# Buffers taken when free, filled waits, and a mask factor on VectorE in place of mask matmuls, in a sparse attention and expert kernel

## The chip, the cores and the metric

The kernel runs on one core of one Trainium2 chip. The metric is the device time of one execution in microseconds (us). Runs that are 1.5 to 3.5% longer than the fastest of the kernel, mostly with a lower granted TensorE clock, are classed as slow and left out of every ratio below.

## The reference, cut to what matters

There are 4 batches, 8 heads, 768 positions, head size 64. Attention is local (a window of 15 positions to either side) plus one entry for each block of 32 keys, whose key is the maximum of the block and whose value is its mean. Its output, 768 x 512 for each batch, goes through a layer of 8 experts; one expert is chosen for a whole batch.

```python
mask_l = np.abs(pos[:, None] - pos[None, :]) < window          # window = 16
scores_l_m = np.where(mask_l, scores_l, -1000000000.0)
scores_all = np.concatenate([scores_l_m, scores_s], axis=-1)    # scores_s: 24 block entries
a = np.exp(scores_all - np.max(scores_all, axis=-1, keepdims=True))
a = a / (np.sum(a, axis=-1, keepdims=True) + 1e-09)
attn = np.matmul(a, np.concatenate([v, v_sum], axis=2))
...
logits = x.mean(axis=1) @ w_gate          # one row for a batch
e_idx = np.argmax(logits, axis=1)         # one expert for a batch
...
h = np.maximum(x[mask] @ w1[e], 0.0)
out[mask] = gate_w[mask, None, None] * (h @ w2[e])
```

Two things follow for the schedule. A batch's expert is known only when its whole attention is done, because the router takes the mean over all positions; only then can that expert's weights (2 MB as they land) be fetched. And a masked score may be made zero after exp as well as very negative before it.

## The kernel before

The program does not issue its work in the order in which it is written. It registers operations with an assumed duration, a priority, the operations they depend on and the buffers they take. A small scheduler, `solve`, plays them through and fixes one order for each engine. That order is what is compiled. A buffer is the oldest in a ring:

```python
for s in op.takes:
    h = hist[s.pool]
    if len(h) >= self.bufs[s.pool]:
        old = h[-self.bufs[s.pool]]            # the one taken longest ago
        if any(u.end is None for u in old.users):
            ok = False
            break
        r = max(r, max(u.end + self.LAT[u.eng] for u in old.users))
```

A score group is one pair of heads and one half of the positions. Four mask matmuls write the bias (0 or -30000) into PSUM, and twelve score matmuls add to it. There are 8 groups for each batch, and one score buffer of two PSUM banks for all:

```python
sc = sc_pool.tile([128, 2, 512], FP32, name="sc", tag="sc")
...
for i, (bias, cs) in enumerate(parts):           # 2 parts x 2 heads = 4 matmuls
    for hh in range(2):
        nc.tensor.matmul(sc[:, hh, cs], lhsT=bias[rs, :], rhs=ident6[rs]...[:, cs],
                         start=i == 0, stop=False, tile_position=(hh * D, 0))
for w in range(NW):                              # 6 windows x 2 heads = 12 matmuls
    for hh in range(2):
        nc.tensor.matmul(sc[:, hh, w * QB : (w + 1) * QB], lhsT=ka[rs, pr, j, :],
                         rhs=qT[rs, j * QB : (j + 1) * QB],
                         start=False, stop=w == NW - 1, tile_position=(hh * D, 0))
```

ScalarE takes the exp (`S_exp`), TensorE multiplies by the values (`O_mm`, tile `ops`), VectorE normalises (`O_norm`), TensorE transposes (`X_mm`, tile `xps`) and ScalarE copies out and sums each row (`X_out`). When all eight groups of a batch are through, the router (`G_mm`, tile `lgps`) multiplies these sums by the gate weights in sixteen matmuls. The expert is `H_mm` (tile `hps`) and `Y_mm` (tile `o_ps`). `V_sum` (tile `vsps`) makes the block means of V; no value product of a batch can run before it.

Before everything else come nine matmuls of zeros (`first_warm`), which are meant to warm the clock. Sixteen transposes took 0.85 us right behind them, at 5.28 us, and 0.53 us at 6.86.

The softmax here doesn't subtract the row's maximum and nothing guards it: scores larger than these inputs give would overflow.

## Time and profile before

| | |
|---|---|
| median of 3 runs (range) | 176.25 us (173.95 to 177.74) |
| profiled run, its span | 175.92 us, 174.2 us |
| granted clock, whole span | 0.901 |
| state of the profiled run | slow |
| fast runs of this kernel in the later calls | 171.4 to 174 us |

TensorE is the engine to look at: it is 87% busy, and the stages in which it is not are the place where something other than its own work decides. The lines of this profile are shown in the prediction.

### The profile page before, as it was taken

What the parts mean: (1) busy time and instruction counts of PE and PEld (TensorE: products, weight loads), DVE (VectorE), ACT (ScalarE), POOL (GpSimd) and SP (SyncE); (2) the same over time, 40 slices, a digit from 0 to 9 for tenths busy, and PEclk for the clock granted to TensorE, in tenths of its full rate; (3) what the DMA queues carried; (4) which work ended last, traced back from release to release, by engine and by line L of the source; (5) the groups of instructions that cost most, each with busy time, mean ns of one, the idle gap of its engine ahead of it and who ended that gap; (6) DMA issues with size and microseconds to landing.
All of it is one profiled execution on the core that took longest, in us unless ns stands there. A gap on an engine that the chain in (4) does not pass through costs nothing.

```text
span 174.2 us, 5138 instructions
## 1 busy us (share of the span) xinstructions
PE 151.6 (87%) x2214; PEld 93.2 (53%) x2225; DVE 83.1 (48%) x224; ACT 100.9 (58%) x204; POOL 45.9 (26%) x62
## 2 busy tenths in 40 slices
PE   6627887495857999989999999999999999999990
PEld 2316766374644555735665657456666544565440
DVE  5991997593396235750885258508644300100000
ACT  2134687677438366866495668563977533485341
POOL 6998300002990009164000090000000370000000
PEclk9965589855597599999999999999999999999999
DMA  3999999990999999999999999981300099990333
GB/s 48 139 138 196 167 206 183 150 56 4 123 161 202 207 194 148 143 198 221 255 245 220 185 147 196 207 234 64 124 0 6 0 122 196 281 243 4 120 121 120
DMA packets 60038, 26.03 MB, mean 149 GB/s; under 512 B 42608, under 2 KB 56944, under 8 KB 60016
## 3 DMA queue, kind: packets, MB, share of 16 engines
q0 software_dynamic: 56032, 19.40, 114.8%
q1 hardware_dynamic: 3984, 6.31, 10.5%
q8 instruction: 17, 0.28, 0.7%
q14 instruction: 5, 0.04, 0.1%
HBM read 38.81 MB, written 6.29 MB: 259 GB/s over the span
## 4 chain that ended last, share of the span: by engine, by line
PE 77%; DVE 12%; ACT 4%; issue 4%; POOL 1%; DVEq 0%; POOLq 0%; ACTq 0%
PE hps L589 25%; PE o_ps L617 24%; PE tps L300 7%; PE sc L411 5%; PE ops L452 4%; PE xps L482 4%; DVE vblk L390 4%; PE sc L423 4%; PE vsps L369 3%; ACT aT L438 3%; DVE xs L469 2%; DVE kmx L328 1%; DVE bind L286 1%; DVE kaug L341 1%; PE lgps L505 1%
## 5 line engine op out<-in xcount | busy, mean ns | idle before, releaser
L589 PE MATMUL hps<-xT,w_sb 128*128 128x384 bf16 x256 | 47.5, 337 | 0.0
L617 PE MATMUL o_ps<-w_sb,hT 128*128 128x512 bf16 x181 | 42.9, 380 | 1.0 <-issue 0.6
L438 ACT ACTIVATE aT<-sc 128x768 bf16<-128x768 f32 x32 | 25.9, 810 | 23.8 <-PE sc L423 23.8
L552 POOL DMA_DIRECT2D w_sb<-in_moe_w_dram x16 | 12.0, 762 | 89.6 <-PE hps L589 53.0
L589 PEld LDWEIGHTS <-w_sb 128*128 128x128 bf16 x256 | 24.4, 101 | 15.9 <-issue 1.5
L608 ACT ACTIVATE hT<-hps 128x384 bf16<-128x384 f32 x53 | 25.2, 492 | 12.7 <-PE hps L589 12.6
L617 PEld LDWEIGHTS <-hT 128*128 128x128 bf16 x192 | 17.4, 98 | 19.4
L636 ACT ACTIVATE o_sb<-o_ps,gcol 128x512 f32<-128x512 f32 x21 | 14.4, 687 | 17.4 <-PE o_ps L617 12.7
L469 DVE TENSOR_TENSOR xs<-ops,rv 128x384 bf16<-128x384 f32 x32 | 17.8, 558 | 1.3
L491 ACT ACTIVATE xT<-xps 128x384 bf16<-128x384 bf16 x32 | 15.5, 493 | 4.9 <-PE xps L482 4.5
L423 PE MATMUL sc<-qT,kaug 64*128 64x64 bf16 x384 | 12.8, 205 | 3.5 <-DVE kaug L347 2.9
L188 POOL DMA_DIRECT2D vblk<-in_v_dram x10 | 15.7, 1576 | 0.5 <-DMA vblk<-in_v_dram 0.5
L606 DVE TENSOR_SCALAR hT<-hps 128x384 bf16<-128x384 f32 x11 | 6.1, 558 | 19.7 <-PE hps L589 19.5
L328 DVE TENSOR_REDUCE kmx<-kaug 128x24 bf16<-128x768 bf16 x16 | 15.0, 947 | 0.9 <-ACT kaug L310 0.9
L411 PE MATMUL sc<-ident,mbias 64*128 64x320 bf16 x64 | 11.2, 346 | 3.3 <-ACT aT L438 3.2
L390 DVE COPY vblk<-vs_sb 24x1536 bf16<-24x1536 bf16 x16 | 11.8, 735 | 4.2 <-ACT vs_sb L310 3.7
L482 PE MATMUL xps<-identb,xs 128*128 128x128 bf16 x96 | 11.1, 245 | 2.9 <-DVE xs L469 2.9
L423 PEld LDWEIGHTS <-kaug 64*128 64x128 bf16 x384 | 9.6, 106 | 5.7 <-issue 3.9
L310 ACT COPY kaug<-tps 128x768 bf16<-128x768 bf16 x11 | 8.8, 799 | 6.3 <-PE tps L300 6.3
L452 PE MATMUL ops<-vblk,aT 120*64 120x65 bf16 x384 | 10.6, 208 | 2.0 <-ACT aT L438 1.4
L300 PE MATMUL tps<-identb,q_nat 96*64 96x96 bf16 x256 | 8.9, 230 | 3.4 <-issue 2.2
L452 PEld LDWEIGHTS <-aT 120*64 120x64 bf16 x384 | 8.6, 121 | 5.3 <-issue 2.3
(74 smaller groups left out, 146.6 us busy)
## 6 DMA issues: line engine op xcount, KB each, us to landing
w_sb<-in_moe_w_dram POOLq DMA_DIRECT2D x12, 512.0 KB, 12.1
out_dram<-o_sb SPq DMA_DIRECT2D x24, 256.0 KB, 5.4
vblk<-in_v_dram POOLq DMA_DIRECT2D x6, 576.0 KB, 21.7
k_nat<-in_k_dram POOLq DMA_DIRECT2D x3, 768.0 KB, 15.3
q_nat<-in_q_dram POOLq DMA_DIRECT2D x3, 768.0 KB, 18.2
vblk<-in_v_dram POOLq DMA_DIRECT2D x2, 564.0 KB, 18.0
w_sb<-in_moe_w_dram POOLq DMA_DIRECT2D x8, 128.0 KB, 5.0
w_sb<-in_moe_w_dram POOLq DMA_DIRECT2D x4, 256.0 KB, 5.9
```

Of the source, the lines that this page charges most:

```text
L300: nc.tensor.transpose(ps[hh * D : (hh + 1) * D, r, :], src[:, 2 * pr + hh, r * D : (r + 1) * D], identb[0:PR, 0:PR],)
L328: nc.vector.tensor_reduce(out=kmxs[b, pr].rearrange("q (j c) -> q j c", c=QB // BLK), in_=kaugs[b % 2][:, pr, :, R_OWN:R_POST].rearrange(" ...
L390: nc.vector.tensor_copy(vblks[b % NV][R_SUM:NR, 2 * pr : 2 * pr + 2, :, 0:D], vss[b, pr][BLK * pr : BLK * pr + NB] .unsqueeze(2) .to_broad ...
L411: nc.tensor.matmul(sc[:, hh, cs], lhsT=bias[rs, :], rhs=ident6[rs].rearrange("p w c -> p (w c)")[:, cs], start=i == 0, stop=False, tile_po ...
L423: nc.tensor.matmul(sc[:, hh, w * QB : (w + 1) * QB], lhsT=ka[rs, pr, j, :], rhs=qT[rs, j * QB : (j + 1) * QB], start=False, stop=w == NW - ...
L438: nc.scalar.activation(aT, scs.pop((b, pr, u))[:, :, 0:HB], ACT.Exp, scale=SCALE)
L452: nc.tensor.matmul(ops[w * QB : (w + 1) * QB, t, hh, :], lhsT=aT[0:NR, hh, c0 : c0 + QB], rhs=vb[0:NR, 2 * pr + hh, u * NW + 2 * t + w, 0 ...
L469: nc.vector.tensor_tensor(out=xs, in0=ops[:, :, :, 0:D], in1=rv.unsqueeze(3).to_broadcast([128, NW // 2, 2, D]), op=ALU.mult,)
L482: nc.tensor.transpose(xps[:, t * 128 : (t + 1) * 128], xs[:, t], identb)
L589: nc.tensor.matmul(hps[:, 0:HB], lhsT=w1_sb[:, dt, ft * 128 : (ft + 1) * 128], rhs=xT[b][:, dt, u * HB : (u + 1) * HB], start=(dt == 0), s ...
L608: nc.scalar.activation(dst, hps[:, 0:HB], ACT.Relu)
L617: nc.tensor.matmul(o_ps, lhsT=hTs[b][:, ft, st * 128 : (st + 1) * 128], rhs=wts[b][1][:, ft, :], start=(ft == 0), stop=(ft == NFT - 1),)
```

## The change

The intent is to take work off TensorE where it is full and to keep its clock up where it is not.

1. In batches 1 to 3 the four mask matmuls of a group go. VectorE multiplies the result of exp by a 0/1 factor instead; two such factors are built once.
2. A buffer is the one that comes free first, and each has its own name.
3. Where the schedule expects TensorE to wait within the first 60 us, matmuls of zeros fill the wait.
4. The router adds its half sums on VectorE first and needs 8 matmuls in place of 16. Batch 1's transposes are held until batch 0's last scores, and some of the assumed durations are new.

```diff
     def solve(self):
-                    h = hist[s.pool]
-                    if len(h) >= self.bufs[s.pool]:
-                        old = h[-self.bufs[s.pool]]
+                    best = None
+                    for i, old in enumerate(held[s.pool]):
+                        if old is None:
+                            t = 0.0
+                        elif any(u.end is None for u in old.users):
+                            continue
+                        else:
+                            t = max(u.end + self.LAT[u.eng] for u in old.users)
+                        if best is None or t < best[0]:
+                            best = (t, i)
 ...
+            op.spare = st - max(room, free.get(eng, 0.0))
 ...
+    def factors(op):                       # seven instructions on VectorE
+        nc.vector.tensor_copy(d_k, it_k)
+        nc.vector.tensor_tensor(out=d_k, in0=d_k, in1=d_k, op=ALU.mult)
+        for i in range(2):
+            nc.vector.tensor_scalar(out=seen[i], in0=d_k, scalar1=float(HALO * HALO),
+                scalar2=None, op0=ALU.is_lt)
 ...
+    def S_mask(b, pr, u):
+        def f(op):
+            rows = aTs[b, pr, u][0:R_SUM]
+            nc.vector.tensor_tensor(out=rows, in0=rows,
+                in1=seen[u].rearrange("p w c -> p (w c)").unsqueeze(1).to_broadcast(
+                    [R_SUM, 2, HB]), op=ALU.mult)
 ...
-            for i, (bias, cs) in enumerate(parts):
+            for i, (bias, cs) in enumerate(parts if b == 0 else []):
 ...
-                        start=False,
+                        start=b > 0 and w == 0,
 ...
+    def G_add(b):                          # reds = the two halves of red, added
 ...
-            for i in range(2 * NP):
+            for i in range(NP):
 ...
+    def warm(op, tile_):
+        if op.start < WARM_UNTIL:          # 60.0
+            for _ in range(int((op.spare - 0.1) / 0.17)):
+                nc.tensor.matmul(tile_, lhsT=zb[:, 0:128], rhs=zb[:, 0:HB],
+                                 start=True, stop=True)
 ...
-        slow_until=24.0, slow=1.8,
+        slow_until=24.0, slow=1.2,
 ...
-    KQ, VV = 1.2, 2.4
+    KQ, VV = 1.1, 2.15
 ...
+        later = [R["S", 0, NP - 1, 1]] if b == 1 else []
 ...
+                if b:
+                    R["e", b, pr, u] = add(
+                        ("dve", 0.5), S_mask(b, pr, u), w - 10, [e, R["fact"]])
```

(The diff is cut to its core. `warm` is called at the head of six of the TensorE operations.)

## The prediction

> **What bounds the kernel now.** I read the busy shares and the 40 slices first, then the chain of work that ended last, then a table of stretches, then the timeline and the DMA issues of the first 62 us. The slices (4.36 us each) show two different kernels:
>
> ```profile
> PE 151.6 (87%) x2214; PEld 93.2 (53%) x2225; DVE 83.1 (48%) x224; ACT 100.9 (58%) x204; POOL 45.9 (26%) x62
> ...
> PE   6627887495857999989999999999999999999990
> ...
> PEclk9965589855597599999999999999999999999999
> DMA  3999999990999999999999999981300099990333
> ```
>
> From about 56 us on TensorE (PE) is at 9 in nearly every slice and its granted clock is full: this part is a sum of PE work. Before that, PE is neither full nor at full clock. The table of stretches (columns: busy us of PE, weight loads, VectorE, ScalarE and GpSimd, each with its count, then granted clock, DMA busy share times length, GB/s) says the same:
>
> ```profile
> 0.00:40.00 40.00, 28.59 (x609) 20.88 (x609) 29.90 (x79) 21.73 (x40) 17.12 (x29) 0.75 1.66 140
> 40.00:62.00 22.00, 16.71 (x291) 11.06 (x288) 11.56 (x32) 12.02 (x29) 9.60 (x10) 0.68 1.00 147
> 62.00:174.20 112.20, 106.35 (x1320) 61.27 (x1329) 41.66 (x114) 67.17 (x136) 19.13 (x23) 1.00 1.17 153
> ```
>
> In the chain (start, us, what) three places matter. One is the serial loop score matmuls, exp, next scores; "L411" are the mask matmuls, "L423" the scores, "L438" the exp. The other two are the same group at full clock, and the router (L505), with which a batch's expert is chosen and its weights may be fetched:
>
> ```profile
> 41.47 0.77 ACT aT L438
> 42.28 0.50 PE sc L411 x4
> 42.78 0.34 PE sc L423 x12
> 43.14 0.82 ACT aT L438
> ...
> 44.82 1.43 PE vsps L369 x36
> 46.28 0.30 DVE vs_sb L312
> ...
> 86.40 0.27 PE sc L411 x4
> 86.67 0.18 PE sc L423 x12
> ...
> 97.74 0.48 PE lgps L505 x16
> ```
>
> There is one score buffer (two PSUM banks), so masks and scores cannot start before the exp has read it. Cold, a turn takes 43.14 - 41.42 = 1.72 us: masks 0.50, scores 0.34, exp 0.81 and hand-overs. Warm, the masks cost 0.27 and the scores 0.18.
>
> The router of batch 0 runs at 39.5 to 40.1 us in the timeline. The expert's first weights are issued at 42.4, its first matmul runs at 46.9, and PE is full from 56. So I split the span as 40.1 us up to the first router and 134.1 us after it. Of the latter, the 40 to 62 stretch has 22.0 - 16.7 = 5.3 us of idle PE, and some 11 us of its busy time ran at half clock, which loses another 5.5 us: about 10.8 us that is not needed work.
>
> [...] the twelve score matmuls take 0.32 to 0.34 us where the granted clock is 0.50 (40 to 46 us) and 0.17 to 0.18 us where it is 1.00. [...] from 36 to 40 us, mostly transposes, PE was busy 4.00 of 4.00 us with a clock of 0.50. [...]
>
> [...]
>
> [...] the 128x176 copies that take 0.20 us later took 1.47 us between 10.6 and 12.1 us, while GpSimd was issuing the V load.
>
> **The change part by part.**
>
> *Mask matmuls.* Four per group, 32 groups before; after, only batch 0's eight groups keep them (the instruction order has 16 + 16 left of 64 + 64). Batches 2 and 3 (16 groups) lie in the saturated part: 16 x 0.27 = 4.3 us. I count 0.20 a group instead, as the mask streams covered some of the twelve weight loads of the scores (0.24 us a group): 16 x 0.20 = 3.2 us.
>
> *Router.* The two half sums are added on VectorE first (about 0.15 us), so 16 matmul passes become 8: 0.24 us off each of the three routers in the saturated part, 0.7 us.
>
> *Batch 1's scores.* These sit in the serial loop. A turn loses its masks: 1.72 becomes about 1.25 us cold, less if warm. In the new order three groups stand ahead of V's sums, all behind the router; in the old one five do, two before the router and three behind it. So V's sums (44.8 us) move earlier with the router and by about another microsecond, and with them the V copies and normalisations that kept PE waiting at 50 to 55 us.
>
> *Fills.* 39 zero matmuls of 128x384, counted in the order: 33 before the first router, six between the third score group of batch 1 and V's sums. At 0.17 us each warm (0.32 cold) they are 6.6 us of PE time (up to 12.5), but each stands where PE is expected to wait anyway. If the waits are as long as planned they cost nothing, and keep the clock up.
>
> *Buffers taken when free, and the order.* Each buffer has its own name now, chosen when it comes free, so a short-lived tile no longer waits for the oldest in the ring. In the profile PE hardly waits for a PSUM buffer by itself; the gain is in the order that this permits. Batch 1's transposes stand after batch 0's last scores. In the old order a q transpose of batch 1 stood before batch 0's last O group and its last two transposes, and PE stood still for 2.2 us before it (31.6 to 33.8), with nothing named that it waited for. The load of q had landed at about 30.2 (13.9 + 16.3), so I suspect the instruction supply behind a full DMA queue, and it may come again.
>
> *VectorE's extra work.* 24 mask products, 24 x 0.47 = 11.3 us; seven instructions that build the factors, about 2 us[...]. They stand ahead of the first copies of K's edges, on the path to the first scores (13.1 us). One more index pattern on GpSimd (the like one took 0.48 us) delays every later load by 0.5. Against it, VectorE loses the first q copy (0.86). I expect the first scores at 13 to 14.5 us: nothing gained, up to 1.4 lost.
>
> *The first router.* V's second half landed at 23.2 us (10.3 + 12.9), q of batch 1 at 30.2; with 0.5 added, 23.7 and 30.7. After V: sums 0.8, copy to SBUF and spread 1.8, then four normalisations of 0.75, a transpose and a copy out, which gives 31. The new order puts all four q transposes of batch 1 (0.46 us each warm, 0.85 cold) before the router: 30.7 + 1.9 to 3.4 + about 1 for what follows, so 33.5 to 36. I take 35.0 in place of 39.5: 4.5 us.
>
> *After it.* Weights landed 3.7 us after issue, issue 2.4 after the router: expert work can start at about 42 rather than 46.9. Its loads take some 11 us more, in which PE has sixteen expert groups and batch 1's rest. Of the 10.8 us lost I expect 7 to remain (about 4 idle, 3 cold): 3.8 us.
>
> *Given back.* In the saturated part O now waits for exp and then VectorE, and VectorE goes from 0.37 busy (41.66 of 112.2) to about 0.45. That is slack enough; I allow 1 us of new idle PE.
>
> Sum: 3.2 + 0.7 + 4.5 + 3.8 - 1.0 = 11.2 us. Span 174.2 - 11.2 = 163.0; the run of that profile took 175.92, so 1.7 is added: 164.7, say 164.5 us.
>
> **The rivals.** (a) *Only PE work counts*: the start stays as it is, because the loads (DMA at 9 in the slices up to 37 us) set the first router, and the gain is 3.2 + 0.7 plus a little: 171. For it: the q load lands at 30 whatever is done. Against: nine microseconds lie between that landing and the router. (b) *VectorE becomes the bound of batch 1*: eight products, the V copies (4.0 us in a row at 46.6), eight normalisations and K's maxima come to some 17 us between 36 and 53; each product also lengthens exp to O. PE would wait about as it does at 50 to 55 now, and the gain shrinks to 7: 168. (c) *The fills are misplaced*: waits are shorter than planned or the clock is cold, and they push real work by up to 6 us, half of it on the path: 168. (d) *The clock stays full from 13 us on*, all slack but 4 us goes: 159.5.
>
> **Range and chances.** 164.5 us, 159 to 170. The saturated part's gain is nearly sure and alone makes over 2% (below 172.7) almost; the start adds to it in all but (a). Faster by over 2%: 0.92; within: 0.07; slower: 0.01.
>
> **What would show it.** Right: the router of batch 0 before 37 us, score groups of twelve matmuls and no masks from batch 1 on, turns of 1.25 us or less, clock above 0.75 in the first 40 us, expert matmuls from 42, PE full from about 50, the product near 0.47 us, router matmuls 0.24. Wrong: a router at 39 or later, clock still 0.5 at 13 to 24 us and 36 to 47, [...] or PE idling over 2 us in the later part behind VectorE.

## The result

The kernel after takes 166.66 us (median of 4 runs, 166.12 to 167.38), against 175.87 us of the kernel before beside it (median of 4 runs, 173.95 to 177.74). A ratio here is the mean time of one kernel's fast runs over that of the other's of the same rounds, so not quite the ratio of the medians quoted. It is 0.951 (0.942 to 0.961): faster. Two more calls, on other chips, ran the same kernel as a control and gave 0.969 and 0.961. The mean of the three is 0.9605, which of the some 173 us of a fast run of the kernel before is 6.8 us. I use this figure, because the first call's runs of the kernel before were among the longest that it had.

The page of the profiled run (166.12 us, span 164.5, a fast run), with the busy shares and the 40 slices of 4.11 us:

```profile
PE 148.9 (91%) x2136; PEld 88.0 (53%) x2136; DVE 96.9 (59%) x264; ACT 99.7 (61%) x199; POOL 46.5 (28%) x63
...
PE   6986989952999999999999999999999999799990
...
PEclk9996599995599999999999999999999999999999
DMA  3999999999999999999999999999500099990333
```

TensorE is at 9 from about 41 us on, where before it reached that at 56. The granted clock is at 9 tenths or more from the start, apart from two slices of 6 and 5 at 12 to 21 us and two of 5 at 37 to 45. Two slices stand out: the 2 at 37 to 41 us, and the 7 at 140 to 144. The table of stretches (columns as in the prediction):

```profile
0.00:40.00 40.00, 31.26 (x626) 20.98 (x627) 29.51 (x90) 23.30 (x42) 19.43 (x33) 0.89 1.91 142
40.00:62.00 22.00, 21.10 (x361) 13.51 (x355) 17.29 (x42) 14.54 (x32) 7.61 (x8) 0.90 1.42 186
62.00:164.50 102.50, 96.58 (x1155) 53.48 (x1155) 50.06 (x134) 61.87 (x126) 19.42 (x23) 1.00 1.24 159
```

From 40 to 62 us only 0.9 us of 22 is idle (5.3 before), and the clock went from 0.68 to 0.90. The rest shrank from 112.2 to 102.5 us. But the two tables are cut at the same times, not at the same work, and fills count as busy, so this is not yet an account. The chain that ended last shows what happens around the first router (L576), with L481 the scores, L496 the exp, L722 the fills, L426 V's sums and L661 the expert:

```profile
34.97 0.35 PE lgps L576 x8
35.32 0.11 issue
35.43 0.23 PE sc L481 x4
35.67 2.64 issue
38.31 0.41 PE sc L481 x8
38.74 0.82 ACT aT L496
39.61 0.52 PE sc L481 x12
40.15 0.82 ACT aT L496
41.01 0.50 PE sc L481 x12
41.51 2.04 PE vsps L722 x6
43.55 1.23 PE vsps L426 x48
...
132.75 11.34 DMA w_sb<-in_moe_w_dram
```

Four readings. The router runs at 34.97 instead of 39.52. Four matmuls into the next score group TensorE stands for 2.64 us, waiting for nothing that the profile names ("issue"). A turn of the serial loop takes 41.01 - 39.61 = 1.40 us. And six matmuls of zeros, at a granted clock of 0.50, stand for 2.04 us right ahead of V's sums. The last line is new: near the end the chain runs through the load of the last expert's weights, and TensorE waits 1.38 us for it:

```profile
144.13 5.37 PE L661 MATMUL hps<-xT,w_sb 128*128 128x384 bf16 x32 [1.38 <-DMA w_sb<-in_moe_w_dram]
```

The product on VectorE, in the groups (busy us, mean ns; then its idle time before them):

```profile
L317 DVE TENSOR_TENSOR aT<-aT,seen 96x768 bf16<-96x768 bf16 x24 | 12.9, 546 | 4.0 <-ACT aT L496 4.0
```

One is recorded with 546 ns. Three in a row took 1.48 us at 55.06 us, so from start to start it is (1.48 - 0.55) / 2 = 0.47 us.

### The profile page after: what moved, and what is told of

The parts are those of the page before. It is cut to its first block, busy times and chain, and to the rows that moved or that the text cites.

```text
span 164.5 us, 5002 instructions
## 1 busy us (share of the span) xinstructions
PE 148.9 (91%) x2136; PEld 88.0 (53%) x2136; DVE 96.9 (59%) x264; ACT 99.7 (61%) x199; POOL 46.5 (28%) x63
## 4 chain that ended last, share of the span: by engine, by line
PE 65%; DMA 15%; POOL 6%; DVE 6%; issue 4%; ACT 1%; POOLq 0%; ACTq 0%
PE hps L661 23%; PE o_ps L689 19%; DMA vblk<-in_v_dram 8%; DMA w_sb<-in_moe_w_dram 7%; PE tps L355 5%; PE sc L481 4%; PE ops L511 4%; PE xps L543 3%; PE vsps L426 2%; DVE vblk L447 2%; POOL k_nat L191 2%; POOL q_nat L191 1%; POOL vblk L202 1%; PE vsps L722 1%; DVE kmx L383 1%
## 5 line engine op out<-in xcount | busy, mean ns | idle before, releaser
L661 PE MATMUL hps<-xT,w_sb 128*128 128x384 bf16 x256 | 47.7, 327 | 1.4 <-DMA w_sb<-in_moe_w_dram 1.4
L689 PE MATMUL o_ps<-w_sb,hT 128*128 128x512 bf16 x192 | 44.4, 380 | 0.0
L496 ACT ACTIVATE aT<-sc 128x768 bf16<-128x768 f32 x32 | 25.9, 808 | 11.8 <-PE sc L481 11.7
L680 ACT ACTIVATE hT<-hps 128x384 bf16<-128x384 f32 x45 | 22.1, 491 | 15.1 <-PE hps L661 14.9
L661 PEld LDWEIGHTS <-w_sb 128*128 128x128 bf16 x256 | 22.8, 98 | 15.1 <-DMA w_sb<-in_moe_w_dram 2.2
L708 ACT ACTIVATE o_sb<-o_ps,gcol 128x512 f32<-128x512 f32 x22 | 15.1, 687 | 16.2 <-PE o_ps L689 13.4
L678 DVE TENSOR_SCALAR hT<-hps 128x384 bf16<-128x384 f32 x19 | 10.6, 556 | 12.1 <-PE hps L661 12.0
L481 PE MATMUL sc<-qT,kaug 64*128 64x64 bf16 x384 | 12.1, 198 | 4.6 <-issue 2.6
L317 DVE TENSOR_TENSOR aT<-aT,seen 96x768 bf16<-96x768 bf16 x24 | 12.9, 546 | 4.0 <-ACT aT L496 4.0
L365 ACT COPY kaug<-tps 128x768 bf16<-128x768 bf16 x13 | 10.0, 795 | 7.8 <-PE tps L355 7.8
L481 PEld LDWEIGHTS <-kaug 64*128 64x128 bf16 x384 | 8.3, 99 | 10.8 <-issue 7.5
L543 PE MATMUL xps<-identb,xs 128*128 128x128 bf16 x96 | 10.7, 220 | 0.6 <-DVE xs L528 0.6
L365 ACT COPY qT<-tps 128x768 bf16<-128x768 bf16 x13 | 9.9, 798 | 2.1 <-PE tps L355 2.0
## 6 DMA issues: line engine op xcount, KB each, us to landing
k_nat<-in_k_dram POOLq DMA_DIRECT2D x3, 768.0 KB, 14.5
```

The costliest lines, as they stand in the source:

```text
L365: nc.scalar.copy(out_, in_)
L496: nc.scalar.activation(aT, scs.pop((b, pr, u))[:, :, 0:HB], ACT.Exp, scale=SCALE)
L543: nc.tensor.transpose(xps[:, t * 128 : (t + 1) * 128], xs[:, t], identb)
L661: nc.tensor.matmul(hps[:, 0:HB], lhsT=w1_sb[:, dt, ft * 128 : (ft + 1) * 128], rhs=xT[b][:, dt, u * HB : (u + 1) * HB], start=(dt == 0), s ...
L680: nc.scalar.activation(dst, hps[:, 0:HB], ACT.Relu)
L689: nc.tensor.matmul(o_ps, lhsT=hTs[b][:, ft, st * 128 : (st + 1) * 128], rhs=wts[b][1][:, ft, :], start=(ft == 0), stop=(ft == NFT - 1),)
```

## The experiments

My theory at this point: the masks give most of the gain, the early router gives several us, and two things give some of it back, the fills and the wait for weights. The rivals: the fills are what matters, through the clock; or the free choice of buffers; or the early router is worth little, because the nameless wait has only moved behind it. Runs were made in three calls, each call on one chip with runs of the kernel before among them.

### First call: one part away at a time

**Without fills.** All fills but the nine at the start are taken away; the order stays.

```diff
-    WARM_UNTIL = 60.0
+    WARM_UNTIL = 0.0
```

> The changed kernel without its 39 fills, every other instruction in the same order. Theory A (the fills carry the start by keeping the clock up): granted clock in the first 40 us falls from 0.89 to about 0.75 as before, batch 0's router comes at 37 us or later instead of 35.3, time 2 us or more above the changed kernel's 166.7. Theory B (the order and the loads carry it: the router waits for V's second half at 24.8 us and the chain behind it): router within 0.7 us of 35.3, time within 1 us of 166.7. The six late fills took 41.5 to 43.5 us just ahead of V's sums, so V's sums should come about 2 us earlier; if PE is then cold, its first 3 us of expert matmuls run at half speed and give that back.

Measured: 164.77 us (163.77 to 167.41), ratio 0.953 (0.942 to 0.964). That is no slower than with fills, perhaps a little faster. The timeline of its profile (162.1 us, a fast run) has the same stretch as the chain above:

```profile
35.06 0.35 PE L576 MATMUL lgps<-wg_sb,reds 128*1 128x8 f32 x8 [0.51 <-DVE reds L567]
...
37.87 0.35 PE L481 MATMUL sc<-qT,kaug 64*128 64x64 bf16 x12 [2.01 <-ACT aT L496]
...
39.56 1.47 PE L426 MATMUL vsps<-vblk,bind 96*32 96x128 bf16 x48
...
41.40 2.74 PE L661 MATMUL hps<-xT,w_sb 128*128 128x384 bf16 x8
```

The router is at the same place, V's sums come 3.9 us earlier (39.56 against 43.48 in the timeline of the kernel after) and the expert 3.6 us earlier. Against that, the first eight expert matmuls run at about half the rate, 2.74 us where the kernel after took 1.47. The nameless wait behind the router is gone; a short one of 0.99 us stands at 31.27 instead. Of theory B the router held, and V's sums gained more than the 2 us that I expected.

But TensorE still waits 2.01 us at that place (37.87), now for exp. On ScalarE three copies of q and the router's own small steps stood ahead of it:

```profile
34.69 2.21 ACT L365 COPY qT<-tps 128x768 bf16<-128x768 bf16 x3
36.74 0.30 ACT L605 ACTIVATE ex<-lg,negm 1x8 f32<-1x8 f32 x1
...
37.04 0.78 ACT L496 ACTIVATE aT<-sc 128x768 bf16<-128x768 f32 x1
```

The kernel after has the same copies there, and its first exp behind the router ran at 38.74 us. So of its 2.64 us the nameless wait cost about 38.74 - 37.04 = 1.7 us; for the rest ScalarE would not have been free. The lead shrinks later: 3.6 us at the expert, 2.0 us at batch 1's router (62.80 against 64.79), 2.4 us at the end of the two profiles.

**Without the late fills.** Only the six ahead of batch 1's V sums are taken away.

```diff
-            warm(op, bank[:, 0:HB])
+            if b == 0:
+                warm(op, bank[:, 0:HB])
```

> Only the six fills ahead of batch 1's V sums taken away. If they lie on the path (V's load landed at 40.2 us, the sums started at 43.5): V's sums at about 41.5 us, time 1 to 2 us below the changed kernel. If their warming pays for them: V's sums earlier, but the clock at 0.5 until about 48 us, time the same within 0.5 us.

Measured: 167.25 us (165.31 to 168.59), ratio 0.959 (0.949 to 0.970) from two fast runs; the other two, the profiled one among them, were slow. In the slow profile V's sums stand at 42.06 us, 1.4 to 1.6 us earlier than in the three profiles with these fills, so the fills were on the path there. Nothing can be told from this of the time, beyond that the six fills don't decide it.

**Masks back.** Order and fills stay as they are, since the plan keeps its durations. Only the instructions change: the four mask matmuls come back in all groups, the products, the building of the factors and the index pattern that it needs go.

```diff
-            for i, (bias, cs) in enumerate(parts if b == 0 else []):
+            for i, (bias, cs) in enumerate(parts):
...
-                        start=b > 0 and w == 0,
+                        start=False,
```

> The changed kernel with the mask matmuls back in all batches and neither factors nor products on VectorE; order and fills unchanged. Theory (mask matmuls cost PE time where it is full): scores with masks 0.44 us against 0.28 alone, 16 groups in the full part, 2.6 us, plus 3 turns of 0.25 to 0.5 us ahead of V's sums: time 2.5 to 4 us above 166.7. Rival (the products on VectorE cost as much by latency as the masks did on PE): time within 1 us of 166.7.

Measured: 171.40 us (170.62 to 173.10), ratio 0.993 (0.981 to 1.004): nearly all of the gain is gone, and the median is 4.7 us above 166.7 where I had expected at most 4. By the ratios (0.9925 - 0.9605) the masks are worth about 5.5 us. Its profile's span is 169.9 us, 5.4 more than that of the kernel after, both in fast runs. As both have the same order, their routers can be compared: those of batches 1, 2 and 3 come 1.86, 3.23 and 5.46 us later (66.65, 97.72 and 133.73 us against 64.79, 94.49 and 128.27). So in this pair the masks cost 1.9 us up to batch 1's router and 3.6 us in the sixteen groups of the next two stages, 0.225 us a group. Against the two later profiles of the kernel after, the second figure is 3.6 and 4.1 us, but the first is only 0.4 and 0.5 us: their router of batch 1 comes at 66.23 and 66.17 us, though their V sums stand within 0.3 us of the first profile's. From 44 to 46 us the granted clock was 0.89 in the first profile, and the first eight expert matmuls took 1.47 us; in the third they took 2.35. So 1.4 us of the 1.9 is the spread of fast runs, and up to the last router the masks cost 4.0 to 5.5 us. One group in the full part, in its timeline:

```profile
107.43 0.31 PE L468 MATMUL sc<-ident,mbias 64*128 64x320 bf16 x2
107.57 0.19 PE L468 MATMUL sc<-ident,mb_end 64*128 64x64 bf16 x2
107.60 0.34 PE L480 MATMUL sc<-qT,kaug 64*128 64x64 bf16 x12
107.87 0.61 PE L688 MATMUL o_ps<-w_sb,hT 128*128 128x512 bf16 x2
```

and one of the kernel after:

```profile
104.03 0.35 PE L481 MATMUL sc<-qT,kaug 64*128 64x64 bf16 x12
104.31 1.04 PE L689 MATMUL o_ps<-w_sb,hT 128*128 128x512 bf16 x4
```

Reckoned from the first start to the next group's start, it is 0.44 us against 0.28. The ends overlap in such lines (the first of these ends at 107.74, the second starts at 107.57), so starts are what to subtract.

**A padded stream.** 24 tiny matmuls of zeros stand behind the nine at the start, where TensorE waits for the first loads anyway. With their weight loads they put 48 instructions ahead of all others.

```diff
         for _ in range(9):
             nc.tensor.matmul(ps, lhsT=zb[:, 0:128], rhs=zb, start=True, stop=True)
+        for _ in range(24):
+            nc.tensor.matmul(
+                ps[:, 0:8], lhsT=zb[:, 0:128], rhs=zb[:, 0:8], start=True, stop=True
+            )
```

> The changed kernel with 24 tiny zero matmuls (48 PE instructions) more at the start. It tests what the 2.64 us of 'issue' in the middle of one score group (35.7 to 38.3 us) is. Theory (supply of PE's instructions, a place in the instruction stream behind a full DMA queue): the wait comes 48 instructions earlier, inside the last q transposes ahead of the router, and the router comes about 2 us later; time up to 2 us above. Rival (a wait for data of that score group): the wait stays in the same score group, router within 0.7 us of 35.3, time within 1 us.

Measured: 167.93 us (167.82 to 169.36), ratio 0.974 (0.965 to 0.982). Its timeline:

```profile
34.44 0.66 PE L355 MATMUL tps<-identb,q_nat 96*64 96x96 bf16 x21
38.32 0.69 PE L355 MATMUL tps<-identb,q_nat 96*64 96x96 bf16 x11 [3.23 <-issue]
38.94 0.35 PE L576 MATMUL lgps<-wg_sb,reds 128*1 128x8 f32 x8
39.22 0.50 PE L481 MATMUL sc<-qT,kaug 64*128 64x64 bf16 x12
```

The nameless wait now stands in the last transposes of q, ahead of the router, and ends at the same time as before, 38.3 us. Between its old place and its new one lie 11 transposes, 8 router matmuls and 4 score matmuls, each with its weight load: 46 instructions, for 48 that were added. So the wait belongs to a place in TensorE's stream of instructions and not to the work that happens to stand there. (The added instructions also put off the first scores, from 11.31 to 13.08 us; by V's second sums, 24.69 against 24.78 us, that is made up.)

Counting the matmuls on record ahead of each such wait in every fast profile makes this sharper:

| kernel | matmuls ahead of a wait, and its length |
|---|---|
| before (slow run) | 479: 2.20 us |
| buffers alone | 479: 2.53 us; 606: 0.36 us |
| factor alone | 479: 2.88 us; 606: 0.54 us |
| no fills | 479: 0.99 us |
| held second weights | 479: 1.62 us |
| after, and its two controls | 606: 2.64, 2.55, 2.67 us |
| masks back | 606: 2.90 us |
| ring buffers | 479: 0.51 us; 606: 2.97 us |
| padded stream | 479: 0.57 us; 607: 3.23 us |

Up to 45 us there are two places only, 127 matmuls apart, 254 instructions with their weight loads. Three shorter nameless waits come later, and they fit the same step: 0.48 us behind 862 matmuls and 1.12 us behind 1886 weight loads in buffers alone, 0.74 us behind 1886 matmuls in masks back. From 606 that is 256 and 1280, 2 and 10 times 128. The waits at 606 end between 38.3 and 39.5 us (40.6 in one kernel); without fills PE gets to matmul 606 only at about 39.5 us and doesn't wait. The queue that the profile names "instruction" moved one packet at about 35.4 us in the kernel after (16 packets and 0.26 MB in the whole span, so some 16 KB each), 2.9 us before the wait ended, and the DMA share stood at 9 tenths until about 38 us. I read this as the supply of instructions, late behind the other loads. That the place is tied to the count is shown. The rest is my reading and not shown: the profile names nothing that TensorE waits for there, and no run took those loads away.

It also tells what fills cost. 33 fills ahead of the first router are 66 instructions more in the same stretch, so they bring the place behind 606 matmuls forward: TensorE reaches it at 35.7 us instead of 39.5, and stands there for 2.64 us where it didn't wait without them.

And it tells what the router's place is worth. In the padded kernel the router stands at 38.94 us, 3.6 to 4.0 later than in the three runs of the kernel after (34.97 to 35.29), but the time is only 0.9738 - 0.9605 = 1.3% longer, about 2.3 us, and batch 1's V sums come 1.3 to 1.5 us later (45.02 against 43.48 to 43.70).

### Second call: one part alone

**The kernel after, again**, as a control on this chip.

> The changed kernel once more, so that the three others of this call have it on the same chip. Every theory expects a ratio of 0.95 to before and a router of batch 0 at 35 us; a score group stopped for 2 to 3 us behind it again[...].

Measured: 167.41 us (166.74 to 168.64), ratio 0.969 (0.960 to 0.978). The span of its profile is 166.7 us, its router at 35.29 us, V's sums at 43.70 us, and the wait for the last weights 1.98 us.

**Free buffers alone.** The kernel before with nothing but the new choice of buffers.

```diff
-    WARM_UNTIL = 60.0
+    WARM_UNTIL = 0.0
...   (masks and sixteen router matmuls as before, no products, no factors)
-        slow_until=24.0, slow=1.2,
+        slow_until=24.0, slow=1.8,
-    KQ, VV = 1.1, 2.15
+    KQ, VV = 1.2, 2.4
-        later = [R["S", 0, NP - 1, 1]] if b == 1 else []
+        later = []
```

> The kernel before with nothing but buffers taken when free (masks on PE, no fills, router of 16 matmuls, no rule that batch 1's transposes wait for batch 0's scores, the old durations in the plan). Theory (its order still has batch 1's q transposes between batch 0's last groups, so the router hardly moves): router at 38 to 40 us, time within 1.5% of before. Rival (free buffers alone bring the early router): router at 36 us, ratio 0.97.

Measured: 172.78 us (171.75 to 174.62), ratio 1.001 (0.987 to 1.015): no difference that these runs can tell. Its profile (span 170.2 us) is useful for another reason. It is a fast profile of a kernel as quick as the one before, which that kernel's own profile is not. It has the first router at 38.68 us, not 39.52, and from 40 to 62 us it has 3.4 us of idle TensorE at a clock of 0.84, where the slow profile has 5.3 us at 0.68. The order is not quite the same, though, and batch 1's V sums stand at the same time in both, 44.76 and 44.75 us, so this shows the state only roughly.

**The factor alone.** The kernel before, ring and order rule as they were, with the factors and the products and without masks from batch 1 on.

```diff
-            for i, (bias, cs) in enumerate(parts):
+            for i, (bias, cs) in enumerate(parts if b == 0 else []):
...
+                        start=b > 0 and w == 0,
...
+                if b:
+                    R["e", b, pr, u] = add(
+                        ("dve", 0.5), S_mask(b, pr, u), w - 10, [e, R["fact"]])
...   (no fills, no new buffers, sixteen router matmuls)
```

> The kernel before with nothing but the mask as a factor on VectorE in batches 1 to 3 (ring buffers, no fills, 16 router matmuls). Putting masks back into the changed kernel cost 5.4 us of span, so theory: ratio 0.965 to 0.975, router of batch 0 at 39 us as before, PE full again from 60 us. Rival (the factor pays only together with the new order): ratio above 0.985.

Measured: 168.99 us (167.42 to 170.27), ratio 0.977 (0.962 to 0.992), about 4 us of the 6.8. The interval is wide; it agrees with the 4.0 to 5.5 us of the masks put back. Its (fast) profile shows something else. It has the old order, and its router runs at 38.69 us; but batch 1's V sums

```profile
43.68 1.47 PE L407 MATMUL vsps<-vblk,bind 96*32 96x128 bf16 x48
```

stand where the kernel after has them (43.48 to 43.70 us), whose router is 3.4 to 3.7 us earlier.

**Ring buffers.** The kernel after, with the buffers taken in turn again.

```diff
+        used = {p: 0 for p in self.bufs}
...
+                    turn = used[s.pool] % self.bufs[s.pool]
                     for i, old in enumerate(held[s.pool]):
+                        if i != turn:
+                            continue
```

> The changed kernel with its buffers taken in turn again, the oldest of the ring, as before. The order up to the first router is the same but for six fills fewer. Theory (PE hardly waits for buffers): router within 0.7 us of the changed kernel's, time within 1% of it. Rival (free buffers matter in the full part): 1.5% or more above it, PE waiting for evacuations after 62 us.

Measured: 167.13 us (166.66 to 169.74), ratio 0.969 (0.957 to 0.981), the same as the control of this call. So as far as these runs can tell (1.2 to 1.4% to either side), the free choice gives nothing by itself, and nothing in company either. The order does change: here the last router stands ahead of all twelve `Y` groups and the wait for the last weights is gone, so what that saves must be lost elsewhere.

### Third call: fills once more, and the end

**The kernel after, a third time**, and **without fills, again**, with six runs each because the difference is small. The edits are none, and the one shown above.

> The changed kernel as control on the chip of this call. Its two earlier sets gave ratios of 0.951 and 0.969 to before; expected 0.96, with PE waiting 1.4 to 2 us for the last expert's weights at about 144 us.

> The changed kernel without its fills, now on the same chip as the changed kernel. Theory (the fills buy a clock that nobody needs before the router, and the late six and the place of the instruction supply cost about 2 us): 1 to 2 us below the control. Rival (the fills pay by the warm clock at 40 to 47 us): equal or above the control.

Measured: 166.19 us (164.94 to 167.03), ratio 0.961 (0.956 to 0.967), and 166.61 us (164.21 to 168.60), ratio 0.959 (0.953 to 0.965). My theory of 1 to 2 us below the control is not borne out: within this accuracy the fills are neutral. In this call all six runs with fills were fast, and of the six without three were slow, the profiled one among them; over all calls the difference is less clear, as the other kernels with fills had slow runs too.

**The second half of the last weights held back.** The idea was that the load of the last expert's first half would land sooner if the second half were issued later, so that the 1.4 to 2.0 us of waiting near the end would go (with no fills).

```diff
             _, t = transfer(G_load(b, 1, 4 * c, 4 * c + 4), 0.8, 2.7,
+                            [R["Y", 2, NST - 1]] if b == 3 else [])
```

> Without fills, and the last expert's second weights issued only when batch 2's last output matmuls are done. It tests what holds up the last chunk of its first weights (landing 11 us after issue). If the second weights share the DMA engines with it: it lands 2 to 3 us earlier, PE's wait before the second half of the last expert's first matmuls (0.65 us without fills, 1.4 to 2 with) is gone. If it is the output stores, or the chunks go in turn anyway: the wait stays, time as without fills.

Measured: 165.57 us (164.75 to 167.91), ratio 0.959 (0.955 to 0.963). This run did not test what it should. A dependency in the plan only orders how operations are emitted; it puts no wait into the program. In its profile the second half was still issued at 132.35 us, right behind the first, and the wait was still there (1.32 us). It counts as a third run of the kernel without fills, and whether holding that load back helps is open.

**The last router first.** Without fills, and with the copy-outs of `H` of the later batches at a lower priority, so that the plan puts batch 3's router ahead of all twelve `Y` groups of batch 2 instead of behind two of them.

```diff
-                o = add(EITHER(0.55, 0.6), H_out(b, ft, u), base - 165, [m],
+                o = add(EITHER(0.55, 0.6), H_out(b, ft, u), base - (165 if b < 2 else 85), [m],
```

> Without fills, and batch 2's expert evictions rank behind batch 3's attention on VectorE and ScalarE, so that batch 3's router stands ahead of all twelve output groups of batch 2 instead of behind two (1.8 us of PE work more to cover the weights' load). Expected: no PE wait for weights at the end, 0.5 to 1 us below the kernel without fills, 2 to 3 us below the control, ratio to before 0.945. Rival (the wait moves elsewhere, PE idles behind evictions between 110 and 125 us): no gain.

Measured: 163.78 us (162.50 to 165.20), ratio 0.949 (0.944 to 0.953). Its profile is of a slow run (span 163.5 us, granted clock 0.896), but the end can be read in it, as the granted clock is 1.00 from 62 us on:

```profile
127.07 0.34 PE L576 MATMUL lgps<-wg_sb,reds 128*1 128x8 f32 x8
...
127.66 10.53 PE L689 MATMUL o_ps<-w_sb,hT 128*128 128x512 bf16 x47
138.03 10.56 PE L661 MATMUL hps<-xT,w_sb 128*128 128x384 bf16 x64
```

All 64 matmuls of `H` run as one piece with no wait. From the router to the first matmul that needs the last piece of the first weights there are now 10.7 + 5.2 = 15.9 us of other work (half of the last `H` among it), where the kernel after had 8.6 + 5.6 = 14.2 us and the kernel before 12.7 + 5.2 = 17.9 us. This kernel beats the control of its call clearly (the intervals 0.944 to 0.953 and 0.956 to 0.967 don't meet), and it is the fastest. Against the two sets without fills of the same call (0.959 and 0.959) it gains 1.0%, some 1.8 us where I expected 0.5 to 1; that is the share of the router's place, and the interval of one of them (0.953 to 0.965) just touches its own.

## Why the prediction was right or wrong

The class and the range held: 166.66 us in 159 to 170, faster. The point was 2.2 us too low, and the gain by fast runs is 6.8 us where my sum was 11.2. That first difference flatters me, as the runs of the kernel before were long that time. Step by step:

- **"Mask matmuls ... 16 x 0.20 = 3.2 us": right**, a little low. Putting them back cost 3.6 to 4.1 us in these two stages, 0.225 to 0.26 a group.
- **"Router ... 0.7 us": right.** A router's matmuls take 0.28 us where they took 0.48, so 3 x 0.20 = 0.6 us.
- **"Batch 1's scores ... 1.72 becomes about 1.25 us cold": nearly.** A cold turn takes 1.40 us. Putting the masks back cost 0.4 to 1.9 us up to batch 1's router, by which profile of the kernel after it is set against. In all the masks are 4.0 to 5.5 us, the largest part of the gain by far.
- **"VectorE's extra work ... first scores at 13 to 14.5": wrong, without consequence.** They run at 11.31 us. The factors took the 2 us that I gave them (7.94 to 10.1 us), but `bind`, just before them, took 0.42 us in place of 1.77. In all the profiles it takes 1.76 to 1.77 us where GpSimd's issue of the V load begins at 5.34 to 5.36 us and 0.41 to 0.42 where the new index pattern has put that off to 5.83 or 5.84. Why is open, as that issue runs on beside `bind` in both cases. And it isn't the whole reason: factor alone has the short `bind` too, and its first scores run at 13.92 us. There a copy of q and two maxima of K stand ahead of the first copies of K's edges on VectorE, as in the kernel before, and in the kernel after one maximum. So the order of VectorE's work decided as well. The product's 0.47 us was an estimate of mine that no row of the kernel before could show, and it was right: 96 x 768 in bf16, with the factor broadcast over the two heads, took 0.47 us from start to start.
- **"The first router ... I take 35.0 in place of 39.5: 4.5 us": right in the time stamp, wrong as a gain.** It ran at 34.97 to 35.29. But the wait I had only suspected "may come again" came again, behind the router instead of in front of it. Moving it to the front in the padded kernel brought the router back to 38.94 us and cost only some 2.3 us. And some 0.8 us of the 39.5 was probably the state of the profiled run (38.68 and 38.69 in fast profiles of two kernels with the old order).
- **"After it ... expert work can start at about 42 ... Of the 10.8 us lost I expect 7 to remain ...: 3.8 us": this is the step that failed.** The expert starts at 45.0 us. Between the router and it stand the 2.64 us of the nameless wait, six fills of 2.04 us on the path, and turns of 1.40 instead of 1.25. Nor had I counted ScalarE: with all four q transposes ahead of the router, three q copies (2.2 us) stood ahead of the first exp, so that even without the nameless wait TensorE waited 2.01 us there. In this kernel the early router was worth nothing to V's sums: factor alone, with its router at 38.69 us, has them at 43.68, the kernel after at 43.48 to 43.70. That PE was full from 45 on, which I expected at 50, did not make up for it, since the fills are part of what fills it. And the 10.8 us was read from a slow profile. By the same rule, and with the clock taken as either full or half, the fast profile of the buffers alone loses 3.4 us to idling and, with a mean clock of 0.84, 32% of its 18.6 busy us at half clock and so some 3.0 us to that: 6.4 us. The kernel after loses 0.9 + 2.1 + 1 to 2 for the late fills (2.0 us, but at half clock, so 1 us of them may be in the 2.1 already) = 4.0 to 5.0 us. These are estimates from the tables, but they say that what was to be won there was about 2 us and not 3.8, and what the masks cost in this stretch is counted in it.
- **"Given back ... 1 us of new idle PE", behind VectorE: the size was near, the cause was wrong.** No wait of that kind shows: weight loads waited 1.1 us for the product in all, and no matmul is on record as waiting for it. What came was a wait of 1.4 to 2.0 us for the last expert's weights, since the new order left little other work between the last router and the expert. That isn't all: in the padded kernel, with the same order and the same 14.2 us, TensorE didn't stop for these weights, and why they landed in time there is open.
- **"Fills ... cost nothing, and keep the clock up": right in sum.** That zeros keep it up was an assumption of mine. The clock of the first 40 us rose to 0.88 to 0.89 with them, against 0.79 to 0.81 in the two fast profiles without, and the time stayed (0.961 with them, 0.959 without). My reason was wrong: they do cost, through the wait behind 606 matmuls that they bring forward and through the 2.04 us. What they earn is shown only in part: of the 3.6 us that the expert starts earlier without them, its first eight matmuls give back 1.3 us (2.74 against 1.47), and 2.0 us are left at batch 1's router in that pair of profiles, though the times hardly differ. And one reading was wrong: from 36 to 40 us, "mostly transposes", these took 1.86 of the 4.00 us, and masks, scores and the router most of the rest. So that stretch is no evidence on what transposes do to the clock; in the run without fills TensorE ran nothing but transposes from 32.26 to 34.5 us, and 32 of them took 0.87 to 0.88 us there, against 1.49 us for 32 at 36.91 us in the kernel before.
- **"Buffers ... the gain is in the order that this permits": wrong.** Alone, and taken out of the whole, they change nothing (1.001; 0.969 beside 0.969).

The sum as measured is 4.0 to 5.5 for the masks and 0.6 for the router, less 1.4 to 2.0 for the last weights, which is 2.6 to 4.7 us (each profile of the kernel after with its own wait); to reach 6.8, some 2 to 4 us are left for the start. I had 4.5 + 3.8 us there, which without the masks' 0.4 to 1.9 us is 6.4 to 7.9. That remainder is a difference and not a measurement: the delayed transposes of batch 1 and the new durations were never tried alone. Masks back leaves 1.3 us net for everything but the masks, the wait for the last weights among it, and its interval includes none.

Of the rivals, (a) was nearest in size: TensorE's own work is most of the gain, although its ground, that the router would stay, was wrong. (b), VectorE as the bound of batch 1, did not show: TensorE idles for 0.9 us from 40 to 62. (c) was half true of the six late fills. (d) fell.

## What to carry to other kernels

Work taken off the engine that is full was paid out nearly one to one here (0.225 to 0.26 us a group for mask matmuls that took 0.27); an event brought forward at the start is paid out only as far as nothing else waits behind it, so follow the path for several steps beyond that event, on the other engines too, before crediting it. Read a loss only from a profile whose state is fast, or take a look at a neutral variant for a second opinion: the kernel without fills has one profile of each state, on two chips, 165.1 us (slow) and 162.1 us (fast). Of these 3.0 us, 2.1 are lost by batch 1's V sums (41.66 against 39.56 us), with a clock in the first 40 us of 0.69 against 0.81; 0.4 us of this is regained by the last router, and 1.2 more are lost in the wait for the last weights (1.88 against 0.65 us). When a wait has no name in the profile, count the instructions ahead of it in several variants: if the count stays and the work changes, as here (606 or 607 matmuls in eight fast profiles of six kernels), the wait belongs to the stream of instructions and not to the work, and instructions added ahead of it bring it forward (48 of them by 46 here).
